# Converting the first MoE's float64 weights: join one turn later, cast two turns behind the sign passes

## The chip, the cores and the metric

The kernel runs on one core of a Trainium2 chip. TensorE is called PE here, VectorE DVE, ScalarE ACT, GpSimd POOL, and SyncE, which issues most of the loads, SP. The metric is the device time of one execution in microseconds (us), given as the median of several runs; the profile is of one execution more.

## The reference

Three stages follow each other: a sparse causal attention (4 batches, 8 heads, 576 tokens, heads of 64), then what the source calls the first MoE, which is a layer norm and a dense MLP with a residual, and then a routed MoE of 8 experts. The change concerns the second stage alone:

```python
def _moe_ref(x, g_ln, w_ch1, w_ch2) -> np.ndarray:
    mu = np.mean(x, axis=-1, keepdims=True)
    var = np.mean((x - mu) ** 2, axis=-1, keepdims=True)
    xn = (x - mu) / np.sqrt(var + 1e-06) * g_ln
    ch = np.maximum(xn @ w_ch1, 0.0) @ w_ch2
    return (x + ch).astype(np.float32)
```

x is 2304 tokens by 512; w_ch1 is 512 x 2048 and w_ch2 is 2048 x 512. [...]

## The kernel before

**Stages.** The attention of batch 0 runs first, alone. Then comes the MLP, over 9 chunks of 256 tokens (c = 0 to 8) and 16 blocks of 128 hidden columns (f = 0 to 15); the attention of the other three batches is threaded into its steps. At each step t of a list `order` the kernel issues `mm1(c, f)` (L645, the hidden block, 12 matmuls) and, one step behind, `mm2` of the step before (L661, 12 matmuls into the accumulators). Both are products of numbers that are split in a high part in fp32r and a rest, three products for each of four depths. Between them stand a relu on ACT (L647) and the rest of the relu's output on DVE (L648). Chunks 0 and 1 run interleaved: (0,0), (0,1), (0,2), (1,0), (0,3), (1,1), (0,4), (1,2) and so on, so (0,f) is at step 2f - 2 and (1,f) at 2f + 3. Batch 1's attention is threaded into steps 8 to 26, in small matmuls to PE (L284, L323, L329, L379, L397) with their copies and softmax on ACT and DVE (L297, L343 to L387, L415).

**Weights.** w_ch1 and w_ch2 are cut into 32 pieces of 512 KB in float64: piece 2f is what mm1 of block f needs, piece 2f + 1 what mm2 needs. Each piece goes through five stages:

- `load_w`: a DMA from SP's queue into a staging buffer (L211), of which there are six (NSTG), in blocks of two pieces;
- `w_low` (L461, DVE): shifts the low words;
- `w_sign` (L467 and L468, ACT): two passes over the high words, the first written as f16, the second an absolute value;
- `w_high` (L473, DVE), called the join: puts both words together to a float32;
- `w_split`: a cast to fp32r (L487, on ACT, for the first four pieces on DVE) and four subtractions on POOL (L490), which give the rest.

The work is planned in turns. Turn k has, in this order, the split of piece k - 2, w_low of piece k, w_sign of piece k - 1 and the load of piece k + 4; the join of piece k - 1 is issued at the end of the same turn. A table sets the four numbers for the last four pieces. The first 6 turns (W_START) are issued during the attention of batch 0. In the MLP, step t issues turns until their number is the larger of W_START + int(WR t) and `need`, which follows from the block f that the step computes (L1073, L1074); with chunks 0 and 1 interleaved, two turns come at each even step, and the last ones at step 26, which computes (0,14). Turns are what the engines' queues are filled from; the scheduling of the framework then sets the order on each engine, and `keep` holds the weight instructions in the order of the program.

**Layer norm.** For chunk 1, `ln_2` (L553 to L557) makes the mean mu on PE, copies it on ACT (L555) and subtracts it on DVE (L557); `ln_4` (L581) makes the variance by 16 matmuls; `ln_split` (L628, L629) makes the operand xc of mm1. `ln_5` (L617 to L621) makes the scale rsb by way of a diagonal dg on DVE, a matmul into ps_rs and a copy on ACT. For chunks from 2 on the mean comes from a sum on POOL (L531, L533), and the squares (L571) alternate with POOL's additions (L572).

Of the kernel before, what the change touches and what calls it, by code (L numbers as in the profile page):

```python
# [50 lines left out]
SPANS = ((8, 26), (36, 54), (65, 86))  # L51

XB, LEAD = 5, 2
W_START, WR, WA, WI, W_DVE = 6, 1.0, 3, 5, 4
LN01, LN_AT, LN_W = (1, 1, 3, 1, 1, 4, 5, 9), (-7, -5, -4), (1, 2, 3, 4)
RT = ((0, 0, 1, 2, 3, 4, 6, 7, 8), (3, 4, 5, 6, 6, 7, 9, 10, 11))
RT_END = (0, 1, 2, 3, 4, 6, 8, 9, 10)
# [15 lines left out]
def attention_moe_moe(ctx: ExitStack, tc: tile.TileContext, q, k, v, g_ln, w_ch1, w_ch2, w_gate, w_local, w1, w2, out):  # L73
# [349 lines left out]
    NW, NSTG = 32, 6  # L423
# [67 lines left out]

    turns, joins = [[] for _ in range(NW + 3)], [[] for _ in range(NW + 3)]
    for i in range(NW):
        ld, lo, hi_, sp_ = i - NSTG + 2, i, i + 1, i + 2
        if i >= NW - 4:
            ld, lo, hi_, sp_ = ((27, 29, 30, 31), (23, 28, 29, 33), (27, 30, 31, 32), (23, 31, 32, 34))[i - NW + 4]
        if wide:
            turns[lo].append((w_low, i))  # L500
            turns[hi_].append((w_sign, i))
            joins[hi_].append((w_high, i))
        turns[sp_].insert(0, (w_split, i))
        if i >= NSTG:
            turns[ld].append((load_w, i))
    nw = [0]

    def weights_turn():
        for fn, i in turns[nw[0]]:
            fn(i)  # L510
        nw[0] += 1
# [3 lines left out]
    def weights_join():  # L515
        while joined[0] < nw[0]:
            for fn, i in joins[joined[0]]:
                fn(i)
            joined[0] += 1

    def weights_next():
        weights_turn()
        weights_join()


    lns, mus, xcs = {}, {}, {}
# [446 lines left out]
    for n in range(2):  # L973
        i = n * (NE + 129)
# [97 lines left out]
    for t, (c, f) in enumerate(order):  # L1072
        need = (2 * f + 4 + 2 * (f == 14) if f < 15 else len(turns)) + WA if t <= last[0] else 0  # L1073
        while nw[0] < min(len(turns), max(need, W_START + int(WR * t))):  # L1074
            weights_next()
# [95 lines left out]
    def tab(n):  # L1171
        cur[0] += n
        return tb[:, cur[0] - n:cur[0]]
# [5 lines left out]
    sn, nx, fl, ld = tab(NTILE), tab(T1), tab(T1), tab(T1)  # L1179
# [455 lines left out]
```

## Time and profile before

| what | value |
|---|---|
| median of 3 runs | 872.39 us (872.22 to 874.93) |
| profiled execution, its time | 872.77 us |
| its span | 870.6 us |
| mean granted clock of TensorE | 0.995 |
| PE busy | 845.5 us, 97% of the span |
| DVE busy | 461.1 us, 53% |
| ACT busy | 353.4 us, 41% |
| POOL busy | 171.8 us, 20% |

The span is what the profile covers; the time has 2.2 us around it in that execution. Busy times are sums over the whole span, in which the stages differ: where ACT is busy 41% over the whole, it has hardly a gap between 52 and 66 us. So a change in the conversion of the weights is read from the stretch in which they are converted, about 52 to 182 us, and in it from the waits that PE has.

### The profile page before, as it was taken

How to read it: one execution, taken by the hardware profiler on the slowest of the kernel's cores; microseconds unless marked ns; L12 is line 12 of the kernel's file. 1: busy time of each engine (PE TensorE's matmuls, PEld its weight loads, DVE VectorE, ACT ScalarE, POOL GpSimd, SP SyncE). 2: the span in 40 equal slices, each digit the busy share in tenths (PEclk: the TensorE clock that was granted, in tenths of full speed). 3: DMA queues.
4: the chain of work that ended last, by engine and by line, in shares of the span. 5: the costliest groups of instructions: out<-in, count | busy, mean ns of one | idle time of the engine just before them, and what ended most of it. 6: DMA issues, size and time to landing. Idle time of an engine off the chain costs nothing. (4 is left out here: it accounts for less than half of the span.)

```text
span 870.6 us, 18870 instructions
## 1 busy us (share of the span) xinstructions
PE 845.5 (97%) x7123; PEld 751.8 (86%) x7130; DVE 461.1 (53%) x1542; ACT 353.4 (41%) x857; POOL 171.8 (20%) x257
## 2 busy tenths in 40 slices
PE   9999899999999999999999999999999999999994
PEld 5688788899999999999999999999888868778773
DVE  4876765558656546666555464675815151121641
ACT  3787876633455233355211222242112252222551
POOL 2245542340120120120211212010032121120111
PEclk9999999999999999999999999999999999999998
DMA  9936352201221102210000000511266175354830
GB/s 192 253 122 202 106 169 74 50 11 54 66 47 42 50 17 59 51 26 16 26 2 26 2 25 1 195 37 38 100 229 243 62 255 213 145 188 169 303 119 23
DMA packets 96547, 87.17 MB, mean 100 GB/s; under 512 B 67378, under 2 KB 75574, under 8 KB 96440
## 3 DMA queue, kind: packets, MB, share of 16 engines
q1 hardware_dynamic: 89256, 69.61, 26.6%
q0 software_dynamic: 3552, 11.11, 3.7%
q10 hardware_dynamic: 3632, 5.09, 1.6%
q8 instruction: 59, 0.97, 0.5%
q14 instruction: 48, 0.39, 0.1%
HBM read 76.27 MB, written 9.97 MB: 99 GB/s over the span
## 5 line engine op out<-in xcount | busy, mean ns | idle before, releaser
L661 PE MATMUL acc<-h,w 128*128 128x256 f32 x1728 | 244.8, 289 | 2.1 <-DVE h L648 1.9
L645 PE MATMUL ps_h<-xc,w 128*128 128x256 f32 x1728 | 236.1, 285 | 0.0
L661 PEld LDWEIGHTS acc<-h,w 128*128 128x128 f32 x1728 | 217.9, 190 | 7.8 <-DVE h L648 3.2
L645 PEld LDWEIGHTS ps_h<-xc,w 128*128 128x128 f32 x1728 | 218.3, 192 | 1.8
L647 ACT ACTIVATE h<-ps_h 128x256 fp32r<-128x256 f32 x144 | 55.9, 389 | 215.7 <-PE ps_h L645 201.9
L648 DVE SCALAR_TENSOR_TENSOR h<-ps_h,h 128x256 fp32r<-128x256 f32 x144 | 60.4, 419 | 96.0 <-ACT h L647 95.5
L87 PE MATMUL ps_y<-wx,ht 128*128 128x512 f32 x336 | 83.8, 399 | 0.0
L490 POOL TENSOR_TENSOR w<-stg,w 128x128 fp32r<-128x128 f32 x128 | 62.5, 521 | 96.4 <-ACT w L487 57.5
L87 PE MATMUL ps_h<-wx,xs 128*128 128x512 f32 x336 | 81.1, 396 | 0.0
L87 PEld LDWEIGHTS ps_h<-wx,xs 128*128 128x128 f32 x336 | 62.7, 188 | 14.9
L87 PEld LDWEIGHTS ps_y<-wx,ht 128*128 128x128 f32 x336 | 61.0, 188 | 12.2 <-issue 0.2
L902 DVE TENSOR_TENSOR xs<-ps_tx,xs 128x512 fp32r<-128x512 f32 x14 | 9.7, 692 | 63.8 <-ACTq L1378 48.1
L1470 ACT ACTIVATE h<-ps_h 128x512 f32<-128x512 f32 x28 | 15.2, 595 | 56.6 <-PE ps_h L87 56.6
L791 DVE TENSOR_TENSOR wx<-raw,wx 128x1024 fp32r<-128x1024 f32 x32 | 37.3, 1217 | 1.3 <-ACT wx L788 1.3
L467 ACT ACTIVATE stg<-stg 128x512 f16<-128x512 f32 x27 | 37.1, 1374 | 0.0
L1484 DVE TENSOR_TENSOR ht<-ps_th,ht 128x512 fp32r<-128x512 f32 x28 | 18.4, 685 | 33.4 <-ACT ht L1483 33.3
L1508 POOL DMA_INDIRECT out_dram<-y,idx x14 | 17.8, 1271 | 90.6 <-ACT y L1507 81.8
L788 ACT CAST wx<-raw 128x1024 fp32r<-128x1024 f32 x32 | 31.8, 1060 | 5.6 <-PE acc L661 5.6
L359 ACT ACTIVATE sm<-sm,st 128x54 f32<-128x54 f32 (+1 forms) x80 | 27.6, 347 | 12.9 <-DVE st L347 12.8
L1483 ACT CAST ht<-ps_th 128x512 fp32r<-128x512 f32 x28 | 15.2, 590 | 36.3 <-PE ps_th L87 36.3
L881 POOL DMA_INDIRECT xg<-xrows,idx x15 | 16.1, 1074 | 53.5 <-issue 19.5
L1507 ACT ACTIVATE y<-ps_y,pr 128x512 f32<-128x512 f32 x18 | 12.4, 690 | 34.4 <-PE ps_y L1497 16.9
(397 smaller groups left out, 1189.1 us busy)
## 6 DMA issues: line engine op xcount, KB each, us to landing
raws<-in_moe_w_dram SPq DMA_DIRECT2D x20, 1024.0 KB
stg<-in_moe_w_ch_dram SPq DMA_DIRECT2D x32, 512.0 KB
raw<-in_moe_w_dram SPq DMA_DIRECT2D x16, 1024.0 KB
xrows<-row ACTq DMA_DIRECT2D x9, 520.0 KB
qnat<-in_q_dram SPq DMA_DIRECT2D x48, 72.0 KB
knat<-in_k_dram SPq DMA_DIRECT2D x48, 72.0 KB
v<-in_v_dram SPq DMA_DIRECT2D x24, 72.0 KB
v<-in_v_dram SPq DMA_DIRECT2D x72, 18.0 KB
```

Of the source, the lines that this page charges most:

```text
L87: return lambda *args, **kw: tc.keep_in_program_order(fn(*args, **kw))
L359: act.activation(sm[0:m, i, :], (ps if mode else sm)[0:m, i, :], AF.Exp, bias=st[0:m, 0, i:i + 1], scale=-1.0, **({} if mode else dict(acc ...
L467: keep(act.activation(t.bitcast(F16)[..., 1], f32(t[..., 1]), AF.Copy, scale=2.0 ** -112))
L490: keep(pool.tensor_tensor(o, x, f32(h), op=ALU.subtract))
L645: pe.matmul(ps, w[:, a, d, o:o + 128], xcs[c][:, b_, d, :], start=(i == 0), stop=(i == 11))
L647: act.activation(h[:, 0, :], ps, AF.Relu)
L648: dve.scalar_tensor_tensor(h[:, 1, :], ps, 0.0, f32(h[:, 0, :]), op0=ALU.max, op1=ALU.subtract)
L661: pe.matmul(accs[c][d // 2][:, d % 2, :], w[:, a, f % 2, d * 128:(d + 1) * 128], h[:, b_, :], start=(f == 0 and (a, b_) == (0, 0) and d % ...
L788: act.copy(wx[i][:, 0, :], raw[i // 2][:, i % 2, :])
L791: dve.tensor_tensor(wx[i][:, 1, :], raw[i // 2][:, i % 2, :], f32(wx[i][:, 0, :]), op=ALU.subtract)
L1484: dve.tensor_tensor(s_[1][:, 4 * g:4 * g + 4, :], ps, f32(s_[0][:, 4 * g:4 * g + 4, :]), op=ALU.subtract)
L1508: pool.indirect_dma_start(out=out, out_offset=bass.IndirectOffsetOnAxis(ap=places(s)[1], axis=0), in_=y, in_offset=None, bounds_check=NT - ...
```

## The change

Three things change: the rate WR is 1.09 for 1.0; in a turn, the joins of the turns before it are issued ahead of its passes and no longer behind them; and the split of a piece comes a turn later, its load two turns later. So turn k now has first the join of piece k - 2, then the split of piece k - 3, w_low of piece k, w_sign of piece k - 1, and the load of piece k + 2. The table for the last four pieces is written anew, and there are 37 turns for 35.

```diff
-W_START, WR, WA, WI, W_DVE = 6, 1.0, 3, 5, 4
+W_START, WR, WA, WI, W_DVE = 6, 1.09, 3, 5, 4
...
-    turns, joins = [[] for _ in range(NW + 3)], [[] for _ in range(NW + 3)]
+    turns, joins = [[] for _ in range(NW + 5)], [[] for _ in range(NW + 5)]
     for i in range(NW):
-        ld, lo, hi_, sp_ = i - NSTG + 2, i, i + 1, i + 2
+        ld, lo, hi_, sp_ = i - NSTG + 4, i, i + 1, i + 3
         if i >= NW - 4:
-            ld, lo, hi_, sp_ = ((27, 29, 30, 31), (23, 28, 29, 33), (27, 30, 31, 32), (23, 31, 32, 34))[i - NW + 4]
+            ld, lo, hi_, sp_ = ((28, 30, 31, 33), (24, 28, 29, 35), (28, 31, 32, 34), (24, 29, 30, 36))[i - NW + 4]
...
     def weights_next():
+        weights_join()
         weights_turn()
-        weights_join()
```

The four numbers of the table are the turns of the load, of w_low, of w_sign (with its join) and of the split, for the pieces 28, 29, 30 and 31. Before, the splits of 28 and 30 stood in turns 31 and 32, which step 24 issues, and those of 29 and 31 in turns 33 and 34 of step 26. Now all four stand in turns 33 to 36, and all these are issued at step 26.

Three places in the order of the engines show it. The first is ACT at the start of the MLP, steps 0 to 2: L555 is the copy of the mean of chunk 1, L628 the passes that make its xc, L487 the cast of a piece, L467 and L468 the two sign passes. Before:

```order
L87 ACTIVATE xc<-xt_379,g_sb 128x256 x4
L487 CAST w_1_869<-stg 128x4x128
L467 ACTIVATE stg<-stg 128x512
L564 ACTIVATE sq_935<-xt_379 128x1024
L468 ACTIVATE stg<-stg 128x512
L647 ACTIVATE h<-ps_h 128x256 x2
L555 COPY mu<-ps_mu 128x256
L487 CAST w_1_897<-stg 128x512
```

And now:

```order
L564 ACTIVATE sq_926<-xt_379 128x1024
L468 ACTIVATE stg<-stg 128x512
L647 ACTIVATE h<-ps_h 128x256
L487 CAST w_1_888<-stg 128x4x128
L467 ACTIVATE stg<-stg 128x512
L647 ACTIVATE h<-ps_h 128x256
L468 ACTIVATE stg<-stg 128x512
L487 CAST w_1_899<-stg 128x512
L467 ACTIVATE stg<-stg 128x512
L555 COPY mu<-ps_mu 128x256
L468 ACTIVATE stg<-stg 128x512
L628 ACTIVATE xc<-xt_419,g_sb 128x256 x4
```

Counted from the four xc passes, the copy of mu had one f16 pass, one abs and one cast ahead of it, and has now three f16 passes, two abs and two casts (one f16 pass, ahead of L564, is not in the piece shown).

The second place is PE at step 26: w_7_2393 and w_7_2555 hold the block of w_ch1 of f = 14 and 15, w_7_2566 that of w_ch2, acc_1110 and acc_1101 are of chunk 1, acc_956 and acc_947 of chunk 0. Before:

```order
L661 MATMUL acc_1110<-h,w_5_1833 128x256 x6
L397 MATMUL ps_o<-pt,v 64x54 x7
L661 MATMUL acc_1111<-h,w_5_1833 128x256 x6
L645 MATMUL ps_h<-xc,w_6_1960 128x256 x5
L397 MATMUL ps_o<-pt,v 64x54
L645 MATMUL ps_h<-xc,w_6_1960 128x256 x7
L619 MATMUL ps_rs<-dg,mean_w 128x256
L645 MATMUL ps_h<-xc,w_7_2393 128x256 x2
L397 MATMUL ps_o<-pt,v 64x54 x3
L397 MATMUL ps_o<-pt,v 64x36 x2
L645 MATMUL ps_h<-xc,w_7_2393 128x256 x10
```

And now:

```order
L661 MATMUL acc_1101<-h,w_5_1835 128x256 x6
L661 MATMUL acc_1102<-h,w_5_1835 128x256 x6
L397 MATMUL ps_o<-pt,v 64x54 x9
L619 MATMUL ps_rs<-dg,mean_w 128x256 x2
L397 MATMUL ps_o<-pt,v 64x54 x3
L397 MATMUL ps_o<-pt,v 64x36 x2
L553 MATMUL ps_mu<-s__2684,mean_w 128x256
L645 MATMUL ps_h<-xc,w_7_2555 128x256 x12
L645 MATMUL ps_h<-xc,w_6_2095 128x256 x12
L661 MATMUL acc_947<-h,w_7_2566 128x256 x4
```

The products with w_7 no longer stand between the parts of ps_o and the ps_rs, but behind all of them.

The third place is ACT at the same step: the copies of the attention's output (L415), the casts of the last pieces and the relus. Before:

```order
L621 COPY rsb<-ps_rs 128x256
L415 COPY xt_468<-ps_o 128x8x6
L415 COPY xt_1809<-ps_o 128x8x4
L487 CAST w_7_2566<-stg 128x512
L487 CAST w_7_2566<-stg_1845 128x512
L647 ACTIVATE h<-ps_h 128x256 x3
```

And now:

```order
L621 COPY rsb<-ps_rs 128x256
L415 COPY xt_468<-ps_o 128x8x6
L415 COPY xt_1799<-ps_o 128x8x4
L487 CAST w_7_2555<-stg 128x4x128 x2
L555 COPY mu<-ps_mu 128x256
L487 CAST w_7_2566<-stg 128x512
L487 CAST w_7_2566<-stg_1848 128x512
L647 ACTIVATE h<-ps_h 128x256
```

Four casts stand there for two, those of pieces 28 and 30 first, and the copy of chunk 2's mean stands between them.

## Rows read from the trace of the kernel before

**Rows 1.** Busy time by stretch: PE, PEld, DVE, ACT, POOL, clock, DMA share, GB/s

```profile
100.00:162.00 62.00, 57.95 (x615) 53.17 (x614) 39.62 (x104) 46.75 (x88) 24.13 (x51) 1.00 0.39 105
...
182.00:202.00 20.00, 20.00 (x165) 19.84 (x164) 15.99 (x50) 7.49 (x21) 4.63 (x4) 1.00 0.01 2
sum 150.00, PE 141.78 PEld 131.73 DVE 96.29 ACT 103.22 POOL 61.53; mean PE 23.63 PEld 21.95 DVE 16.05 ACT 17.20 POOL 10.25
```

**Rows 2.** Waits from 52 to 182: engine, line, releaser: us, times, longest

```profile
ACT w L487 <- DVE stg L473: 9.4, 13, 1.8
...
DVE stg L461 <- DMA stg<-in_moe_w_ch_dram: 0.8, 1, 0.8
```

**Rows 3.** Timeline of ACT, 56 to 62: start, length, line, operands, idle before

```profile
56.76 0.38 ACT L555 COPY mu<-ps_mu 128x256 f32<-128x256 f32 x1
57.66 0.67 ACT L487 CAST w<-stg 128x512 fp32r<-128x512 f32 x1 [0.52 <-DVE stg L473]
58.24 1.37 ACT L467 ACTIVATE stg<-stg 128x512 f16<-128x512 f32 x1
59.34 0.50 ACT L297 ACTIVATE qT<-ps_tr 128x288 f32<-128x288 f32 x1
59.75 0.67 ACT L468 ACTIVATE stg<-stg 128x512 f32<-128x512 f32 x1
60.31 1.29 ACT L628 ACTIVATE xc<-xt,g_sb 128x256 fp32r<-128x256 f32 x3
```

**Rows 4.** Timeline of PE in steps 0 to 8

```profile
57.00 1.84 PE L581 MATMUL ps_var<-mean_w,sq 128*128 128x1 f32 x16
58.70 0.44 PE L284 MATMUL ps_tr<-iw,qnat 96*128 96x96 f32 x3
...
65.84 1.46 PE L661 MATMUL acc<-h,w 128*128 128x256 f32 x10 [0.46 <-DVE h L648]
...
72.67 1.58 PE L661 MATMUL acc<-h,w 128*128 128x256 f32 x11 [0.93 <-DVE h L648]
...
75.52 1.98 PE L661 MATMUL acc<-h,w 128*128 128x256 f32 x12
77.34 1.60 PE L645 MATMUL ps_h<-xc,w 128*128 128x256 f32 x12
```

**Rows 5.** Timeline of PE in the middle, its longest waits

```profile
97.00 0.53 PE L379 MATMUL ps_pt<-iw,sm 128*96 128x128 f32 x3 [1.13 <-DVE sm L368]
...
105.39 0.47 PE L284 MATMUL ps_tr<-iw,qnat 96*128 96x96 f32 x3 [1.34 <-ACT pt L387]
...
128.35 0.47 PE L284 MATMUL ps_tr<-iw,knat 96*128 96x96 f32 x3 [1.58 <-ACT qT L297]
```

**Rows 6.** Timeline of PE around step 26

```profile
163.76 1.70 PE L645 MATMUL ps_h<-xc,w 128*128 128x256 f32 x12
...
181.06 1.60 PE L645 MATMUL ps_h<-xc,w 128*128 128x256 f32 x12
182.50 1.60 PE L661 MATMUL acc<-h,w 128*128 128x256 f32 x12
```

**Rows 7.** Timeline of ACT and of DVE around step 26

```profile
172.53 0.29 ACT L415 COPY xt<-ps_o 128x72 f32<-128x72 f32 x1 [0.93 <-PE ps_o L397]
173.22 0.25 ACT L415 COPY xt<-ps_o 128x48 f32<-128x48 f32 x1 [0.41 <-DVE xt L415]
...
176.13 0.47 DVE L617 TENSOR_SCALAR dg<-iw,va 128x128 f32<-128x128 f32 x2
```

**Rows 8.** Timelines of POOL and DVE: subtractions of a piece and of the mean

```profile
58.41 3.10 POOL L490 TENSOR_TENSOR w<-stg,w 128x128 fp32r<-128x128 f32 x4 [2.87 <-ACT w L487]
74.00 1.76 POOL L490 TENSOR_TENSOR w<-stg,w 128x128 fp32r<-128x128 f32 x4 [2.46 <-ACT w L487]
...
58.55 1.76 DVE L557 TENSOR_TENSOR xt<-xt,mu 128x512 f32<-128x512 f32 x2
186.84 1.29 DVE L557 TENSOR_TENSOR xt<-xt,mu 128x512 f32<-128x512 f32 x2
```

## What the change should do to the time

> **What bounds the kernel now.** I read the windows first. From 52 to 182 us, while the MLP's float64 weights are still being converted, TensorE (PE) works 121.8 of 130 us, that is the 141.78 of the sum less the 20.00 of the last window; from 182 us, when the last piece has gone, it is busy 20.00 of 20.00 us [rows 1]. So the change can act on 8.2 us of waits at most for a gain, and whatever it saves or loses ahead of 182 us goes straight to the end, because behind it PE never waits for long enough to give it back. The granted clock is 1.00 from 100 to 162 us, the 2.4 GHz level, although PE waits 1.34 and 1.58 us at a time there [rows 1, 5]; so I cost nothing for the clock.
>
> Next, the waits. The casts on ACT (L487) wait thirteen times for DVE's join (L473), 9.4 us in total [rows 2]: these are the waits that the change is made against. ACT is not what the end hangs on, but PE's waits name ACT's products: the transposes wait 1.34 us for pt and 1.58 us for qT, the probabilities' transpose waits 1.13 us for sm [rows 5]. Then the timeline of ACT, where I look for what stands between a weight pass and a layer norm copy [rows 3], and that of PE, where I look for the places at which products of the MLP stand still [rows 4, 6].
>
> **Planned turns.** The factor 1.09 does nothing by itself. At each step the number of turns is the larger of 6 + int(WR t) and of `need`, which at step t is t + 9 or t + 8; 6 + int(1.09 t) is below both up to the last step concerned, 26. Two turns come at each even step as before, and the last turns at step 26. Costed at nothing. What the change does is the offset: a piece is split a turn later, its load is issued two turns nearer to its first use, the join stands at the head of the next turn; and pieces 28 and 30, whose splits stood at step 24, are split at step 26, where mm1(0,14) wants piece 28.
>
> **Start, steps 0 to 8.** On ACT the copy of mu for chunk 1 now has two more f16 passes, an abs and a cast ahead of it. By the starts of the next instruction these take 1.10 us (58.24 to 59.34), 0.56 (59.75 to 60.31) and 0.58 (57.66 to 58.24) [rows 3]: 2 x 1.10 + 0.56 + 0.58 = 3.3 us, so mu goes from 56.76 to about 60.1. The subtractions of mu (1.76 us) and the splitting passes behind it shift by as much, but those of before had slack, so that I leave mm1(1,0) at its old time. What had filled PE's time ahead of it, the sixteen variance matmuls and three transposes [rows 4], 1.84 + 0.44 = 2.28 us, is still to be done behind it: +2.28. New waits of products for relu passes that stand behind an f16 pass or a cast: I put one of each, 1.10 + 0.58 less the time that PE has other work, 1.1 us. Against this go waits of before which fall in the same place: 0.46 and 0.93 us, and two products of 12 matmuls which took 1.82 us to the next one (75.52 to 77.34, and one more like it) where the same product takes 1.44 us (181.06 to 182.50) [rows 4, 6], together 0.46 + 0.93 + 0.76 = 2.15. Sum +1.2. Bounds: 0 if the new waits are hidden, +2.3 if the old ones stay.
>
> **Middle, steps 9 to 24.** Here the join, ready at the next turn's head, is done before ACT gets to the cast, and ACT loses no time before it. PE's three long waits for ACT's chains are 1.13 + 1.34 + 1.58 = 4.05 us [rows 5]; ACT's own 9.4 us [rows 2] are larger, so they could all go. But each of these has another chain (softmax on DVE, transposes on PE) in it, which I cannot shorten, and ACT's queue at that place is only partly weights. I take 60%: -2.4. Bounds -4.05 and -0.8 (one short wait less).
>
> **End, step 26.** This is where I expect the loss. Before, in 163.76 to 181.06, 17.3 us, PE had eight products of 1.44 us, 11.5, and 3.3 us of small matmuls (ps_o, ps_pt, ps_rs): 14.8, and 2.5 us of waits [rows 6]. After, the order on PE puts all ps_o, both ps_rs and ps_mu ahead of mm1(0,14), which waits for the cast of piece 28, and that cast stands on ACT behind the copies of the last ps_o:
> - ps_rs waits for the copy that frees its bank, and the second one for dg behind the first: 0.5 + 0.6, estimated from a copy of 0.25 and a dg of 0.47 us with the crossings between engines [rows 7];
> - the copies of a ps_o took from 172.53 to 173.47, 0.94 us, three in turn on ACT, DVE, ACT; the cast follows, 0.67 by 57.66 [rows 3]: 1.6 us, in which PE has a single matmul, ps_mu, 0.3: 1.3 us [rows 7];
> - mm1(0,14) takes its last four matmuls from POOL's subtractions, 1.76 us a piece where its first eight last 1.0: with what DVE adds to it, below, 0.95;
> - mm2(0,14) waits for the relu, which stands behind the casts of pieces 29 and 31, and 29's goes into the room of the stage of 28 and 30, so behind both pieces' subtractions. From the first cast: 2 x 1.76 + 1.0 (DVE beside POOL) + 0.7 + 0.55 + 0.8 = 6.6, in which PE has two products and the stall above, 4.1: 2.5 us;
> - relu(0,15) behind three squares which alternate with POOL's additions: 0.5.
>
> Together 6.35, less the 2.5 of before: +3.9. Bounds +2.4 (POOL undisturbed, no ps_rs wait) and +4.9.
>
> The 1.0 us is from rows: four subtractions took 1.76 us alone and 3.10 us beside the two subtractions of mu, +1.34, which take DVE 1.76 us then and 1.29 us without POOL [rows 8]; not all of it falls at the same time here, so I take 1.0. The Trainium skill's page "SBUF — State Buffer" (section "SBUF: two separate sides") has it that DVE with two inputs in SBUF and GpSimd share a port pair which the first to start holds for its whole instruction. The trace agrees: one after the other would be 1.76 + 1.29 = 3.05 us, measured 3.10. By that rule the full 1.3 us would fall due, and the time would be 875.4.
>
> **Sum.** +1.2 - 2.4 + 3.9 = +2.7 us. The profiled execution took 872.77 us with a span of 870.6, so it stands 0.4 above the median of 872.39; on the median, 872.4 + 2.7 = 875.1. A measurement here can tell about 0.3%, 2.6 us, from no change, so this lies at that edge.
>
> **Rivals.**
> 1. The gains cancel the losses: 872.4. For it: bounds of the three terms overlap (0 - 4.05 + 2.4 = -1.65; 2.3 - 0.8 + 3.9 = +5.4), and the copy of mu is only one of four chains at the start. Against: the stand at step 26 is fixed by the order.
> 2. Faster by more than can be measured. The mechanism is ACT's wait for the join, 9.4 us: if PE's long waits of steps 9 to 24 all come from it, -4.05 falls in full; the start then gains as well, -0.5, since the casts there wait for the join too (0.52 us at 57.66 [rows 3]); and the end costs +1.5, the time being taken from ps_rs and ps_mu work already done: 869.4. It decides if ACT's queue is ahead of PE at 97, 105 and 128 us.
> 3. Loads come late. A piece is loaded two turns ahead of its w_low, not four; a piece such as 23 or 27 stands on SP's queue behind loads of v and k which wait for their buffers. DVE's queue stands behind w_low, and ACT and PE behind DVE. Before, DVE waited once for such a load, 0.8 us [rows 2]. Two turns take two steps, some 9 us here (130 us for 27 steps), and I found no load that stands behind its use, so this needs a landing that is long, which a queue full of v and k at step 14 to 22 could give. If two or three come 2 us late, +4.5 on top of the forecast: 879.6.
>
> **Chances.** The forecast (873.4 to 877.0) 0.44, of which a quarter lies within 0.3% of before; rival 1 0.28; rival 2 0.18; rival 3 0.10. Faster 0.19, within 0.3% 0.38, slower 0.43. The range goes from 869.4, half of rival 2, to 878.4, which leaves out most of rival 3.
>
> **What would show it.** In the profile of the changed kernel: the casts' wait for joins gone from 9.4 us to under 3 (else the offset does not do what it says); mu of chunk 1 copied near 60 us and the variance matmuls behind mm1(1,0); the waits of 1.13, 1.34 and 1.58 us gone or shorter; between the last ps_o and mm1(0,14) a stand of over 1 us that ends with a cast, and before mm2(0,14) one of over 2 us that ends with DVE's h or ACT's relu; PE busy 100% for 20 us behind it. DVE's w_low waiting for a load over 1 us in total would speak for rival 3. I am wrong in the step at the end if PE finds mm1(0,14) ready, and in the middle if those three waits stand as they did.

## The result and the profile after

The changed kernel takes 877.5 us (median of 5 runs, 876.3 to 878.6) where the kernel before takes 872.5, also the median of 5: 5.0 us more. The ratio over all runs is 1.0052, with an interval of 1.0041 to 1.0062 that leaves out 1, so it is slower. The forecast was 875.1, 2.7 us more, so its sign was right and its size was about half of what came. The profiled execution took 877.5 us with a span of 875.6 and a mean granted clock of 0.989; before, 870.6 and 0.995. The two spans differ by 5.0 us as well, so they can be laid side by side.

The best reading for that is the lateness of one and the same matmul: its start in the trace after, less its start in the trace before. PE's small matmuls outside the MLP stand in the same order among themselves in both, so the n-th of a line is the same one; each of those below has as many matmuls of PE ahead of it in both traces.

```
matmul (start before)          late after, us
ps_tr   L87    10.70              +0.6
ps_o    L87    42.50              +0.6
ps_tr   L284   82.27              +1.7
ps_sc   L323   91.87              +4.3
ps_pt   L379   97.00              +3.0
ps_tr   L284  128.35              +1.3
ps_o    L397  162.58              +1.0
ps_x    L681  189.11              +5.7
ps_tr   L284  348.36              +6.0
ps_tx   L888  640.84              +5.1
```

The first 0.6 us are not the change's: they arise in the first 7 us of the execution, ahead of all that was changed, and other executions do not have them (e9 and e10 below are 0.1 late there). The change itself then loses at the start, gets most of it back in the middle, and loses 4.7 us between 162 and 189 us, which nothing gives back until the third stage (there PE waits 1.09 us for a gather that it waited 1.77 us for before). That is the shape that was forecast, start, middle and end. What the forecast did not have stands in the column of the clock. Windows of the changed kernel (stretch, length, busy time with instructions of PE, PEld, DVE, ACT, POOL, granted clock, DMA share, GB/s):

```profile
84.00:86.00 2.00, 1.17 (x11) 0.96 (x9) 1.38 (x3) 2.00 (x4) 1.64 (x4) 1.00 0.27 61
86.00:88.00 2.00, 1.39 (x12) 1.39 (x13) 0.99 (x3) 0.56 (x2) 0.28 (x1) 1.00 0.38 86
...
92.00:94.00 2.00, 2.00 (x14) 2.00 (x13) 1.90 (x10) 1.60 (x3) 0.52 (x2) 0.62 1.00 372
94.00:96.00 2.00, 2.00 (x12) 2.00 (x11) 2.00 (x7) 1.35 (x2) 2.00 (x3) 0.52 0.06 23
96.00:98.00 2.00, 2.00 (x24) 1.70 (x23) 2.00 (x8) 1.69 (x3) 0.69 (x3) 1.00 0.04 8
...
172.00:174.00 2.00, 0.81 (x3) 0.44 (x4) 0.68 (x3) 0.61 (x2) 0.00 (x0) 1.00 0.32 74
174.00:176.00 2.00, 1.35 (x12) 0.87 (x12) 0.34 (x2) 0.27 (x2) 0.00 (x0) 0.60 0.03 8
...
178.00:180.00 2.00, 2.00 (x10) 1.91 (x10) 1.21 (x2) 0.37 (x1) 2.00 (x4) 0.50 0.00 0
...
182.00:184.00 2.00, 1.55 (x11) 1.16 (x10) 0.42 (x1) 1.74 (x6) 1.91 (x5) 1.00 0.00 0
```

From 84 to 88 us PE is busy 2.56 of 4 us; from 92 to 96 the granted clock is mostly at its lower level, 1.2 GHz for 2.4, although PE is busy all the time by then and would have used it. A longer low stretch follows the stand of 172 to 174. In the kernel before the clock stood at 1.00 in all windows from 52 to 202 us [rows 1 shows two of them].

PE of the changed kernel, timeline (start, length, line, operation, operands, count, idle time before it and what ended it), the rows that answer to [rows 4 to 6]:

```profile
62.57 0.38 PE L645 MATMUL ps_h<-xc,w 128*128 128x256 f32 x1 [0.74 <-ACT xc L628]
...
64.83 1.84 PE L581 MATMUL ps_var<-mean_w,sq 128*128 128x1 f32 x16
...
74.51 1.58 PE L661 MATMUL acc<-h,w 128*128 128x256 f32 x11 [1.60 <-DVE h L648]
...
83.66 0.41 PE L284 MATMUL ps_tr<-iw,qnat 96*128 96x96 f32 x3
...
86.61 0.47 PE L284 MATMUL ps_tr<-iw,knat 96*128 96x96 f32 x3 [1.44 <-ACT qT L297]
...
93.71 2.57 PE L645 MATMUL ps_h<-xc,w 128*128 128x256 f32 x12
...
172.52 0.70 PE L619 MATMUL ps_rs<-dg,mean_w 128*128 128x256 f32 x2 [0.89 <-ACT xt L415]
173.89 0.68 PE L619 MATMUL ps_rs<-dg,mean_w 128*128 128x256 f32 x2 [0.67 <-DVE dg L617]
...
177.12 1.22 PE L553 MATMUL ps_mu<-s__2684,mean_w 128*128 128x256 f32 x2 [1.77 <-POOL s__2684 L533]
177.78 4.75 PE L645 MATMUL ps_h<-xc,w 128*128 128x256 f32 x24
182.91 2.03 PE L661 MATMUL acc<-h,w 128*128 128x256 f32 x12 [0.37 <-ACT h L647]
```

The variance matmuls stand behind mm1(1,0), which begins at 62.57, now, as foreseen. The waits that stood out in [rows 5] (1.13, 1.34 and 1.58 us) are 0 and under 0.9 us here, but new ones of 1.60 and 1.44 us stand at 74.5 and 86.6. The product at 93.71 takes 2.57 us where 12 matmuls took 1.60 in [rows 6]; the 24 matmuls of mm1(0,14) and mm1(1,12), from 177.78, take 4.75 for 2 x 1.44 + 0.16 = 3.04.

ACT, in timeline at both places, and of the waits the one that [rows 2] begin with:

```profile
60.48 0.46 ACT L555 COPY mu<-ps_mu 128x256 f32<-128x256 f32 x1
...
85.62 0.65 ACT L468 ACTIVATE stg<-stg 128x512 f32<-128x512 f32 x1
86.18 0.38 ACT L297 ACTIVATE qT<-ps_tr 128x288 f32<-128x288 f32 x1
...
176.05 1.22 ACT L487 CAST w<-stg 128x512 fp32r<-128x512 f32 x2
...
181.36 1.22 ACT L487 CAST w<-stg 128x512 fp32r<-128x512 f32 x2 [2.60 <-POOL w L490]
182.48 0.37 ACT L647 ACTIVATE h<-ps_h 128x256 fp32r<-128x256 f32 x1
```

```profile
ACT w L487 <- DVE stg L473: 1.5, 1, 1.5
```

ACT's waits for joins went from 9.4 us to 1.5, so the change does what it says. What ACT does with the time is the point: from 62 to 86 us it has hardly a gap between its passes, and the copy of qT, which PE waits for at 86.61, is started only at 86.18, behind an absolute value, a relu, an f16 pass and a cast. In the kernel before, ACT and PE at the second group of q's transposes:

```profile
68.09 0.39 ACT L297 ACTIVATE qT<-ps_tr 128x288 f32<-128x288 f32 x1
69.02 0.69 ACT L487 CAST w<-stg 128x512 fp32r<-128x512 f32 x1 [0.53 <-DVE stg L473]
```

```profile
64.89 0.41 PE L284 MATMUL ps_tr<-iw,qnat 96*128 96x96 f32 x3
```

There the copy fell into a stretch in which ACT would otherwise have waited longer for a join. The order on PE changed too: these transposes stand at 83.66 now and not at 64.89, right ahead of those that need their copy done.

### The profile page after: what moved, and what is told of

It reads as the page before. It is cut to its first block, busy times and chain, and to the rows that moved or that the text cites. A ratio compares the mean times of both kernels' runs of the same rounds, so it can differ in the third digit from the quotient of the medians.

```text
span 875.6 us, 18876 instructions
## 1 busy us (share of the span) xinstructions
PE 848.9 (97%) x7123; PEld 755.4 (86%) x7130; DVE 464.8 (53%) x1542; ACT 354.0 (40%) x857; POOL 179.0 (20%) x257
## 5 line engine op out<-in xcount | busy, mean ns | idle before, releaser
L645 PEld LDWEIGHTS ps_h<-xc,w 128*128 128x128 f32 x1728 | 220.9, 194 | 3.4 <-ACT xc L628 0.9
L490 POOL TENSOR_TENSOR w<-stg,w 128x128 fp32r<-128x128 f32 x128 | 70.1, 580 | 86.9 <-ACT w L487 44.1
L467 ACT ACTIVATE stg<-stg 128x512 f16<-128x512 f32 x27 | 37.4, 1386 | 0.6 <-DVE stg L461 0.6
```

The costliest lines, as they stand in the source:

```text
L467: keep(act.activation(t.bitcast(F16)[..., 1], f32(t[..., 1]), AF.Copy, scale=2.0 ** -112))
L490: keep(pool.tensor_tensor(o, x, f32(h), op=ALU.subtract))
L645: pe.matmul(ps, w[:, a, d, o:o + 128], xcs[c][:, b_, d, :], start=(i == 0), stop=(i == 11))
```

## The experiments

All kernels here are edits of a few lines; of the table of the last four pieces the four numbers of each are shown. Lateness is always against the trace of the kernel before.

**The changed kernel with the last four pieces as before but for their loads (e1), and the kernel before with the changed table of the last four pieces (e2).** Among what this moves are the two splits of pieces 28 and 30, back to step 24 in e1 and on to step 26 in e2; the low and sign passes and the other two splits move with them, so what is tested is the table as a whole. Together the two part the end from all the rest: e1 has the changed kernel's order on PE, and e2 that of before, up to about 163 us.

```diff
 # e1, from the changed kernel
-  ((28, 30, 31, 33), (24, 28, 29, 35), (28, 31, 32, 34), (24, 29, 30, 36))
+  ((28, 29, 30, 31), (24, 28, 29, 33), (28, 30, 31, 32), (24, 31, 32, 34))
 # e2, from the kernel before
-  ((27, 29, 30, 31), (23, 28, 29, 33), (27, 30, 31, 32), (23, 31, 32, 34))
+  ((28, 30, 31, 33), (24, 28, 29, 35), (28, 31, 32, 34), (24, 29, 30, 36))
```

> The changed kernel, but pieces 28 and 30 are split in turns 31 and 32 again, which step 24 issues. Theory: the stand before and in mm1(0,14) is made by these two splits alone, and it is 4.4 us of the changed kernel's loss (PE's lead over the kernel before goes from 1.3 to 5.7 us late between 160 and 195 us). Then this kernel stands 4.4 below the changed one, at 873.1, with the granted clock at 1.00 from 162 to 188 us, and PE 1.3 us late throughout. Rival: the end gives way in the same places because the weights as a whole come a turn later (also 29 and 31, the copies of ps_o); then it stays above 876.

> The kernel before, with the changed table for pieces 28 to 31 alone. Theory: the end's loss needs nothing of the rest of the change: +4.4, 876.9, with no product of w_ch1's last block ahead of the last ps_o, a wait of ps_mu for POOL of over 1 us, and the clock at its lower level after it. Rival: the end's loss comes with the weights' later turns and PE recovers here behind the kernel before's waits: 872.5 to 874.

e2 took 878.1 us (877.1 to 881.1), 1.0069 times before (1.0042 to 1.0096). Its PE is 0.2 us ahead at 128 us and 4.7 late at 189, with the granted clock at 0.50 from 176 to 182 us: the end's loss needs nothing of the rest of the change. PE in its timeline at the place:

```profile
171.99 0.70 PE L619 MATMUL ps_rs<-dg,mean_w 128*128 128x256 f32 x2 [0.99 <-ACT xt L415]
173.36 0.67 PE L619 MATMUL ps_rs<-dg,mean_w 128*128 128x256 f32 x2 [0.67 <-DVE dg L617]
...
175.99 1.22 PE L553 MATMUL ps_mu<-s__2684,mean_w 128*128 128x256 f32 x2 [1.50 <-POOL s__2684 L533]
176.65 5.59 PE L645 MATMUL ps_h<-xc,w 128*128 128x256 f32 x24
```

These are the same waits as in the changed kernel, down to a tenth or three of a us. e1 took 874.3 us in the median of ten runs, 1.0015 times before (1.0003 to 1.0026): 3.2 us less than the changed kernel, where 4.4 were expected. But its runs lie far apart, from 872.0 to 877.5, and they lie nearly in the order of the granted clock:

```
time     872.0 872.7 873.3 873.8 874.3 874.4 875.1 875.2 876.0 877.5
span     870.0 870.7 871.3 871.9 872.3 872.4 873.1 873.3 874.1 875.6
clock    0.996 0.995 0.994 0.993 0.993 0.994 0.992 0.992 0.991 0.989
```

One and the same program differs by 5.6 us in its span, as much as the whole effect of the change, with a clock that differs by 0.007. Its profiled execution is the one of 877.5 us, the slowest. A wait of 1.76 us for a copy of the attention's output is new in it, and the clock is low behind that. Its PE row and its windows:

```profile
168.44 0.62 PE L379 MATMUL ps_pt<-iw,sm 128*54 128x128 f32 x4 [1.76 <-ACT xt L415]
```

```profile
91.00:96.00 5.00, 5.00 (x30) 4.84 (x29) 4.38 (x18) 3.01 (x5) 2.54 (x4) 0.66 0.54 186
162.00:170.00 8.00, 6.24 (x67) 5.53 (x65) 4.60 (x13) 6.15 (x11) 4.42 (x9) 1.00 0.07 15
170.00:174.00 4.00, 4.00 (x24) 3.62 (x21) 0.33 (x1) 1.23 (x4) 0.00 (x0) 0.57 0.19 43
```

The two low stretches cost 5 x 0.34 and 4 x 0.43, 1.7 us of full clock each, 3.4 together; its lateness is 0.7 at 162 us and 3.2 at 189. So the table of before is no free end under the changed order either: it costs 2.5 us there in this execution, where the changed table costs 4.7. In the median the change without its table is still 1.9 us slower than the kernel before; its fastest run is as fast as the fastest of before (872.0 and 871.9), but no profile of such a run shows what it is like inside. The theory on the end stands, by e2; the expected clock of 1.00 and the even 1.3 us of lateness do not.

**The join first alone (e3), the offset alone (e4).** e3 is the kernel before with `weights_join()` ahead of `weights_turn()`; e4 is the changed kernel with the two in the old order.

```diff
 # e3, from the kernel before; e4 is the reverse, from the changed kernel
     def weights_next():
+        weights_join()
         weights_turn()
-        weights_join()
```

> The kernel before, with the join at the head of the next turn and nothing else: the cast comes right behind the join of the same piece, so ACT still waits for it, but no longer for the w_low that stood ahead of the join. Theory: it is the distance between join and cast that takes ACT's waits away, so they stay over 5 us here (9.4 before, 1.5 in the changed kernel) and the time stays within 0.3% of before, 871 to 874. Rival: the join's place alone carries the middle's gain of 2.9 us: 869.5.

> The changed kernel with the join at the end of its turn again, so only the split a turn and the load two turns later. Theory: ACT has no waits for joins here either, runs its weight passes without a gap from 53 to 86 us, and PE waits for its copies as in the changed kernel, so 876 to 878. Rival: the join's new place on DVE makes the start's loss (DVE did join, w_low, join, w_low from 71.9 to 74.1 us ahead of the rest that PE waited 1.60 us for); then that wait goes and the time is 875 or less.

e3 took 877.6 us (1.0053, 1.0033 to 1.0072), e4 879.9 (1.0079, 1.0059 to 1.0098). For e3 the mechanism came as expected and the time did not: the waits of the casts for joins are longer than before, not shorter,

```profile
ACT w L487 <- DVE stg L473: 14.3, 21, 1.8
```

and PE waits 1.49 us for kT at 88.7 and 1.84 for qT at 131.9, each followed by a stretch at the lower clock (92 to 96 and 132 to 137 us), and 1.35 and 1.51 us at 152.6 and 172.3, which were not. e4 has no wait for joins; it waits 1.09 and 1.53 us for relus at 69 and 80 us, the clock is low from 81 to 85, from 91 to 95 and at the end. So the wait of 1.60 us is gone where the join is back in its old place, as its rival said, but others came for it, and the time is the worst of the four. Neither half of the change is good by itself; which of PE's small matmuls waits changes with every edit, and that one waits does not.

**The changed order from piece 16 on only (e5), and up to piece 15 only (e6).**

```diff
 # e5, from e1 (join first in turns from 17 on)
-        ld, lo, hi_, sp_ = i - NSTG + 4, i, i + 1, i + 3
+        ld, lo, hi_, sp_ = (i - NSTG + 2, i, i + 1, i + 2) if i < 16 else (i - NSTG + 4, i, i + 1, i + 3)
 # e6, from the changed kernel, with the last four of before (join first in turns up to 17)
-        ld, lo, hi_, sp_ = i - NSTG + 4, i, i + 1, i + 3
+        ld, lo, hi_, sp_ = i - NSTG + (4 if i < 22 else 2), i, i + 1, i + (3 if i < 16 else 2)
```

> The order of before for pieces 0 to 15, the changed one (join first, split a turn and load two turns later) from piece 16 on, and pieces 28 and 30 split at step 24. Theory A: the changed kernel's middle is a true gain (from 98 to 160 us PE made good 2.9 us against the kernel before, since ACT no longer waits for joins); with the start and the end of before it remains: 869.5. Theory B: the middle only gives back what the start had lost, because the chains there (softmax, loads) set PE's pace in both kernels: 872.4. A drop of the granted clock adds about 1.7 us to either.

> The reverse: the changed order for pieces 0 to 15, that of before from 16 on and at the end. Theory A (middle a true gain): the start's loss of 4.3 us stays to the end, 876.5. Theory B (the middle gives the start back in any order): 1 to 1.5 us remain, 873.7. The end shows no stand before mm1(0,14) in either.

e5 took 878.6 us (1.0053, 1.0031 to 1.0075), with runs from 872.7 (clock 0.995) to 882.1 (0.983), so 869.5 is out of reach: no run of twelve was under the median of before. Up to 97 us it has the order of before on PE, ACT, DVE and POOL. Even so its clock was low from 89 to 93 us, where the kernel before and e2 with the same order had it at 1.00; the last wait of over 0.3 us ahead of that was one of 0.93 us at 72.5, as in the kernel before.

```profile
89.00:90.00 1.00, 1.00 (x8) 1.00 (x8) 0.13 (x1) 0.97 (x3) 0.64 (x2) 0.63 0.88 353
90.00:91.00 1.00, 1.00 (x6) 1.00 (x6) 1.00 (x3) 0.50 (x2) 0.00 (x0) 0.50 0.23 94
```

It made PE 0.8 us late at 92 us, and at 97 us PE was 0.4 ahead again: the wait of 1.13 us for sm, which stands there in the kernel before [rows 5], did not occur. Behind that, in the changed order, comes the longest wait of all kernels here, with the clock low behind it:

```profile
104.67 0.47 PE L284 MATMUL ps_tr<-iw,qnat 96*128 96x96 f32 x3 [2.05 <-ACT pt L387]
```

```profile
102.00:106.00 4.00, 1.95 (x18) 1.74 (x16) 3.90 (x9) 4.00 (x7) 3.29 (x6) 1.00 0.59 162
106.00:118.00 12.00, 11.48 (x81) 10.05 (x81) 5.59 (x14) 5.57 (x12) 3.68 (x7) 0.57 0.52 136
```

12 x 0.43 is 5.2 us of full clock. Here too ACT runs ahead while PE waits: at 102 to 106 us ACT is busy 4.00 of 4.00 and PE 1.95. At step 26 e5 has e1's wait again (1.75 us at 171.4) and the clock low behind it. e6 does not compute the same result, and its third stage is other work; its time of 920 us says nothing, and only the stretch up to 350 us, which has the same instructions, is read. On ACT it has the changed order up to 97 us, on PE up to 105. It is 4.2 us late at 92, 2.9 at 97, and 1.9 at 128, at 162 and at 189 us, with the clock low from 92 to 96. So between 97 and 162 us the order of before also gives back part of the loss, 1.0 us, where the changed one gives back 2.0 (+3.0 to +1.0). And the 1.3 us that both make good between 92 and 97 us is what e5 made good there in the order of before. At most half of what the middle gives back is the change's; the rest is only that PE, when late, waits less.

**PE kept busy in the two waits of the start (e7).**

```diff
 # from the changed kernel: in mm2(0,3) behind its first matmul, 13 times, and behind mm1(0,5), 20 times
+    pe.matmul(accs[c][0][:, 0, :], idle[:, 0:128], idle[:, 0:256], start=False, stop=False)
```

> The changed kernel with 13 and 20 matmuls of zeros that add nothing to the accumulators, placed on PE where it waited 1.60 us (74.5) and 1.44 us (86.6); other work is as it was. Theory: the fall of the granted clock to 0.50 from 92 to 96 us follows from these waits; with PE kept busy it stays at 1.00 there and the product (0,6) takes 1.6 us instead of 2.6, so PE is 1.0 us less late at mm2(1,3), and the time is 876.5. Rival: the clock falls at 92 us all the same, and the time is 877.5 or more.

The clock stayed up, as its windows show:

```profile
92.00:94.00 2.00, 2.00 (x19) 2.00 (x20) 0.72 (x4) 0.19 (x1) 0.00 (x0) 1.00 0.56 211
94.00:96.00 2.00, 2.00 (x19) 1.98 (x17) 1.93 (x10) 2.00 (x3) 1.11 (x3) 1.00 0.00 0
```

as the theory has it; one execution does not prove it, since e9 and e10, below, had the clock up with the waits in place. And the time went up, to 881.3 us (1.0095, 1.0079 to 1.0110): the zeros ran past the waits (the 20 took 2.36 us for a wait of 1.44, and PE is 4.6 us late at the matmul that stands at 82 us before), at 97 us it is 2.9 late, as the changed kernel is, and further waits of 2.4 us for DVE and 0.9 us for loads of k come behind 190 us and one more stretch of low clock at 600. What the clock gave, the filling took.

**The end taken apart (e8, e9, e10).** In e8 the subtractions of pieces 28 and 30 run on DVE; in e9 chunk 2's mean is planned a step later, which takes ps_mu from its place ahead of mm1(0,14); e10 has both.

```diff
 # e8 and e10, from the changed kernel
-            keep(pool.tensor_tensor(o, x, f32(h), op=ALU.subtract))
+            keep((dve if i in (28, 30) else pool).tensor_tensor(o, x, f32(h), op=ALU.subtract))
 # e9 and e10
-            for t, fn in zip(LN_AT if c > 2 else (-3, -2, -1), (ln_1, ln_2, ln_3)):
+            for t, fn in zip(LN_AT if c > 2 else (-2, -1, -1), (ln_1, ln_2, ln_3)):
```

> The changed kernel, but the eight subtractions of pieces 28 and 30 run on DVE, which is idle there, and no longer on POOL, so the casts of 29 and 31 and the relu of (0,14) do not wait for POOL. In the changed kernel mm2(0,14) waited 0.4 us for that relu, although the two products ahead of it ran at the lower clock (24 matmuls in 4.7 us, 2.2 more than at the full one). Theory: the low clock and POOL's chain lie side by side, so taking one away leaves the other: the wait goes, mm2(0,14) is 0.6 us earlier, 876.9. Rival: POOL's chain is the whole of it, as the prediction had it (2.5 us): 875.

> The changed kernel with the mean of chunk 2 planned one step later, so that ps_mu no longer stands on PE ahead of mm1(0,14). Theory: it was ps_mu behind POOL's addition (1.77 us of wait) and not the cast of piece 28 that held PE: mm1(0,14) begins 1.0 us earlier, right behind the cast; of this the end keeps 0 to 0.8, because mm2(0,14) still waits for the relu behind POOL's chain: 876.7 to 877.5. Rival: the cast was the last to come in any case, and nothing moves at mm1(0,14).

> Both edits together. Theory: neither POOL's chain nor ps_mu is left, so PE's products follow each other from the cast of piece 28 on: 1.7 us earlier than the changed kernel if the clock falls to 0.50 there all the same (875.8), 3.5 earlier if it does not (874). Rival: the waits for ps_rs and the copies of ps_o, which stand, are most of the end's loss: over 876.5.

They took 876.7, 877.9 and 876.5 us (1.0043, 1.0065 and 1.0047; intervals of 1.0026 to 1.0082 in all), four runs each. None of the three can be told from the changed kernel's 877.5 (876.3 to 878.6) by its time, so what follows is read from one trace of each. PE's rows behind the last ps_o, e8 first:

```profile
177.90 4.47 PE L645 MATMUL ps_h<-xc,w 128*128 128x256 f32 x24
182.21 2.24 PE L661 MATMUL acc<-h,w 128*128 128x256 f32 x12
```

then e9:

```profile
172.86 0.85 PE L397 MATMUL ps_o<-pt,v 54*64 54x54 f32 x10
175.13 5.13 PE L645 MATMUL ps_h<-xc,w 128*128 128x256 f32 x24 [1.42 <-ACT w L487]
180.40 2.04 PE L661 MATMUL acc<-h,w 128*128 128x256 f32 x12
```

and e10:

```profile
175.19 5.13 PE L645 MATMUL ps_h<-xc,w 128*128 128x256 f32 x24 [1.42 <-ACT w L487]
```

In e8 the wait ahead of mm2(0,14) is gone and it comes 0.7 us earlier, as expected, with the 24 matmuls at the low clock: that and POOL's chain lie side by side. (By 189 us e8 is as late as the changed kernel, 5.8 us; a product behind it waits for DVE instead.) In e9 mm1(0,14) follows the cast by its own wait, 1.42 us: 2.3 us behind the start of the last ps_o group, where in the changed kernel it was 3.3 (174.50 to 177.78). So ps_mu was the last to come, by 1.0 us, and the cast right behind it in rank. The product that begins at 181.06 in the kernel before [rows 6] begins at 187.65 in the changed one, at 185.15 in e9 and at 184.47 in e10; less what each was late at 162 us (1.0 late, 0.6 and 0.6 ahead) this stretch costs 5.6, 4.7 and 4.0 us. So at this product ps_mu's place is worth 0.9 and POOL's chain 0.7, and most of the loss is in what e10 still has: the two waits for ps_rs, the 1.42 us and 24 matmuls at the low clock. That was e10's rival. And even the 0.9 and 0.7 do not last, because e9 and e10 still have the mean of chunk 2 to make, which the changed kernel has done by then: at 348 us the three are 6.0, 5.2 and 4.6 us late, so from 162 us to there they lost 4.9, 5.8 and 5.1 us (e8 5.2).

e9 and e10 tell one more thing that was not asked. They have the order of the changed kernel, of e1 and of e8 on PE, ACT and DVE through the start and nearly all of the middle, and their profiled executions had the clock up there; those of the other three had it low for a stretch between 91 and 96 us. Here are e9's windows at that place:

```profile
84.00:86.00 2.00, 0.65 (x6) 0.44 (x4) 1.38 (x3) 2.00 (x4) 1.75 (x4) 1.00 0.47 106
...
92.00:94.00 2.00, 2.00 (x19) 2.00 (x17) 1.93 (x10) 2.00 (x3) 1.06 (x3) 1.00 0.60 239
94.00:96.00 2.00, 2.00 (x24) 1.70 (x23) 2.00 (x7) 1.88 (x5) 1.55 (x3) 1.00 0.04 8
```

Its waits are the same (1.59 and 1.44 us), its lateness is not: 0.9 us at 97 for 3.0, and 0.6 us ahead of before at 162 us, for 1.0 late. Not all of that is the clock's. Laid beside e9, matmul by matmul, the changed kernel is 0.5 us behind from the first 8 us on and still 0.5 at 92 us, 2.0 at 97 and 1.6 from 105 to 162 us. So the fall of the clock took 1.5 us, of which 0.4 were made good by 105, and is worth 1.1 us at 162. e1 and e8, laid beside e9 in the same way, give 0.2 to 1.3 and 0.3 to 1.4: 1.1 us each. Whether the fall comes is not settled by the order.

## Why the prediction was right, and where its size went wrong

The terms, as forecast and as the traces show them. The forecast counted the wait of 1.13 us at 97 us to the middle, so the start is read up to the matmul at 91.87 in the kernel before:

```
                                           forecast   measured
first 7 us, ahead of all that changed         0         +0.6   (changed kernel)
start, to 92 us                             +1.2        +2.1   (e9, e10, clock up)
middle, 92 to 162 us                        -2.4        -2.8   (e9, e10)
clock, low between 92 and 96 us               0         +1.1   (changed kernel, e1 and e8 beside e9)
end, step 26                                +3.9        +4.7   (changed kernel, 162 to 189 us)
behind 189 us                                 0         -0.7   (changed kernel)
sum                                         +2.7        +5.0
```

So the shape was right, and the size fell short by 2.3 us in four places: the clock, the start, the end, and 0.6 us of one execution with which the change has nothing to do. Behind 189 us 0.7 us came back that nobody had counted on.

- **The clock** is the term that was put at nothing and should not have been. "I cost nothing for the clock" rested on the kernel before, in which waits of 1.34 and 1.58 us left it at 1.00 [rows 1, 5]. That was true of that one execution and is no rule: it fell in four of the six profiles that have the changed kernel's order at this place (changed kernel, e1, e6 and e8, not e9 and e10), and in one of the three that have the order of before (e5, not before and e2). So the fall is not shown to be the change's doing, though it came more often with it. It cost 1.1 us at 162 us in the changed order and nothing at 97 us in e5, where the wait behind it took it up. The second low stretch, of step 26, is contained in the +4.7; all seven profiles with the changed table have it. One low stretch took between 1.7 and 5.2 us of full clock in these profiles.
- **The factor 1.09** does nothing, as said: 6 + int(1.09 t) is at no step from 0 to 26 above the turns that `need` has called for by then. No kernel with 1.0 alone was run.
- **Start.** The copy of mu came at 60.48 (forecast 60.1), the variance matmuls behind mm1(1,0), mm1(1,0) at 62.57, no later than before (63.08), and the lateness in step 8 was 1.4 us in the changed kernel (mm1(0,5) at 82.21 for 80.83) and 0.9 in e9, near the 1.2. The wait of 1.44 us for qT right behind that was not foreseen, and it is what makes 2.1 of it: I had taken each pass to be late by what stood ahead of it and had not asked what ACT does once its waits for joins are gone, which is to get ahead with weights.
- **Middle.** The size is near, -2.8 for -2.4, and the waits of [rows 5] are shorter, as forecast; the cause is half of what I took it for. The wait of 1.13 us at 97 us is not ACT's: its row names DVE. It went because PE came late to it, as it did in e5 in the order of before, and with it 1.3 of the 2.8 us. Behind 97 us e6 shows that 1.0 us would have been given back in the order of before as well, and e5 that the same order in another place costs more than it brings. So this term was a guess at 60% whose size came out by luck in good part.
- **End.** The size is near, +4.7 for +3.9, and e2 shows that the new numbers of the last four pieces alone make it. The waits for ps_rs were forecast as 0.5 and 0.6 and were 0.89 and 0.67. That mm1(0,14) waits for the cast was wrong in rank: ps_mu, which waits for POOL, came 1.0 us later still (e9). And the 2.5 us ahead of mm2(0,14) were 0.4, because the two products ahead of it ran at the low clock, 1.7 us longer; it began at 182.9, 6.2 us behind the first cast's end at 176.7, where 6.6 was forecast. So the forecast chain had its length, with PE slow instead of idle beside it; e8, which shortens it, is no less late at 189 us, so it is not alone in setting the end.
- **DVE beside POOL.** The subtractions of pieces 28 and 30 took 4.30 us beside the two subtractions of the mean, which took 1.80, and those of 29 and 31 took 3.43 without any:

```profile
177.03 4.30 POOL L490 TENSOR_TENSOR w<-stg,w 128x128 fp32r<-128x128 f32 x8
182.09 3.43 POOL L490 TENSOR_TENSOR w<-stg,w 128x128 fp32r<-128x128 f32 x8 [0.76 <-ACT w L487]
```

```profile
178.79 1.80 DVE L557 TENSOR_TENSOR xt<-xt,mu 128x512 f32<-128x512 f32 x2 [2.31 <-ACT mu L555]
```

  That is 0.9 us more on POOL for the 1.0 forecast. By the Trainium skill's page "SBUF — State Buffer" (section "SBUF: two separate sides"), whoever starts first holds the shared ports for its whole instruction, which would make it 1.29 us, the full length of DVE's two, and 3.43 + 1.29 = 4.72 for POOL's eight. The measured 4.30 lies 0.4 us below that, so here part of DVE's work ran beside POOL's; in the kernel before, 3.10 us for 3.05 [rows 8], it had fitted.
- **Rivals.** Loads that come late: in the waits of the changed kernel from 52 to 182 us no engine waits for a load of weights, so this one did not occur. That the gains cancel the losses holds at 162 us with the clock up (e9 is 0.6 us ahead there), and for the change without its table in e1's fastest runs, but not for the whole. The faster one needed the full 4.05 us of the middle, of which 2.8 came.

What stays open: why the clock falls in one execution of an order and not in another. At steps 0 to 8 the runs show it low behind waits of 1.60 and 1.44 us in some executions and not in others, up in one execution in which these two waits were filled (e7), and low once in the order of before, where PE had been busy but for small waits since 72.5 us (e5). Clock and span go together over the runs of e1 and of e5; what tips it was not tried. Nor was it tried what the two waits for ps_rs are worth at the end, which stand in all kernels with the changed table that were profiled.

## What to carry to other kernels

A wait of an engine that is not the bottleneck can be the gap into which other work fits: taken away, a queue in fixed order lets the work with the most slack (here the weights, wanted two turns later) run ahead of the copies that the bottleneck engine needs next. The traces of the changed kernel show this at the one copy of qT; it is no rule that fewer such waits are worse, since e3, in which ACT's casts wait 14.3 us for 9.4, came out as slow. Before moving the last pieces of a pipeline nearer to their use, list at that very step what else the engine has in front, here the copies of the attention's output, the mean's sum on POOL and the casts. Where TensorE is near full, put a bound on the clock (here 1.1 us for one low stretch, nothing where a wait stood behind it) and do not rest on one execution in which it stayed up. And before two traces are subtracted, look how far apart they are ahead of all that was changed, here 0.6 us, and take several runs with their clocks before a few us are believed.

## What the runs showed of the hardware that was not expected

- One program's runs spread by 5.6 us in e1 and by 9.4 us in e5 (spans of 870.7 to 880.1), nearly in the order of their mean granted clock, 0.996 to 0.989 in e1 and 0.995 to 0.983 in e5. Per 0.001 of mean clock that is about 0.8 us, and 0.001 of an 870 us span is 0.87, so over whole runs the two go almost one for one. A single low stretch can cost less: the changed kernel's first took 1.5 us, of which 1.1 were left at 162 us, and e5's first took 1.0 us, of which nothing was left at 97 us.
- A low stretch began after PE had been busy again for several us: in the changed kernel the waits are at 84 to 88 us and the clock falls behind 92 us, with PE busy 8.00 of 8.00 us from 88 to 96. It falls on the products behind, not on the wait: 12 matmuls took 2.57 us for 1.60.
- Waits that are alike had unlike results: 1.44 us at 86.6 in the changed kernel (low from 92 to 96), 1.44 us at 86.1 in e9 (up until step 26), 1.58 us at 128.4 in the kernel before (up from 52 to 202 us). And in e5 the clock fell at 89 us with no wait of over 0.3 us since 72.5.
